# fp32 products on four column quarters, in a new order of operations: attention with memory, then a soft mixture of experts, on one core

## The chip, the core and the metric

The kernel runs on one core of a Trainium2 chip. The metric is the device time of one execution in microseconds. Before the change three runs gave 528.36, 534.36 and 540.67 us; the median is 534.36 us. One further execution was taken by the profiler and is the source of every row shown here.

## The reference

Everything is fp32. There are 8 batches, 8 heads, 576 positions and 64 features per head; then 8 experts of 4 slots each with a hidden width of 1024.

```python
scores = q @ k.T / 8, causal mask, softmax  -> a           # per (batch, head)
local  = a @ v
q_p    = where(q > 0, q, exp(q) - 1) + 1
mem    = (q_p @ M_prev) / (q_p @ z_prev + 1e-6)
attn   = sigmoid(beta) * mem + (1 - sigmoid(beta)) * local
x      = attn as (4608, 512)                               # heads side by side
logits = x @ phi                                           # 32 slots
d      = softmax of logits over the 4608 rows              # dispatch
slot_input = d.T @ x
slot_out[e] = relu(slot_input[e] @ w1[e]) @ w2[e]
out    = softmax of logits over the 32 slots @ slot_out    # combine
```

## The kernel before

**Attention.** Each of 32 iterations `n` handles one batch and a pair of heads, the two heads on the two halves of the 128 partitions. `loadq`, `loadk`, `loadv` and `loadm` fetch its inputs. `qhi`/`qlo` and `kn`/`kl` split q and k into a rounded part and a rest, from which `s.q1`, `s.q2` and `s.q3` make scores in three single-pass products (line 433, contraction over 64 partitions for each head). The blocks at the ends of the sequence, `s.a`, `s.b`, `s.z` and `s.zb`, are true fp32 products (line 427) with a stationary operand of 128 x 128. `max.*` (DVE, line 462) masks, scales and moves scores out of PSUM and finds the row minimum, `exp.*` (ACT) does the exponential with its sum, `t.*` transposes the result on the tensor engine (line 560), `te.*` moves the transposes out of PSUM into the tile `at`, and `av.*`/`memb` multiply by v (line 598), the two heads as two products with 64 columns each, side by side on the array.

**Memory part.** `qmin`, `qexp`, `qphi` make q_p. `norm` (line 518) makes its product with z, in four column quarters already. `neps`, `nmk`, `nred` work out the reciprocal in a form of 128 rows; `nrw` writes it to DRAM (line 540) and `nrr` reads it back, broadcast over rows, into the tile `rb` (line 546); `qn` (DVE, line 550) multiplies. `mema` multiplies by M (lines 592 and 593). In the same manner `rec`, `rt`, `rte` make the softmax reciprocal, `rrw` writes it to DRAM (lines 491 to 493), `rrr` reads it back as `rr`, a part of the tile `rm` (line 497), and `mo` (line 626) and `xe.*` (lines 633 to 637) combine everything into `xt`.

**Mixture.** For each block of 512 rows the operations `x1` to `x5` make logits, running maximum, dispatch sums and combine weights; `y*` is the last block and the hand-over. Then come the expert products `f1` and `f2` (lines 932 and 949, stationary operands of 32 columns, four experts side by side) and `comb` (line 1006), which also stores the output.

**What sets the order.** One string, `SEQ`, lists 2546 operations in program order, with the PSUM bank of each product after a colon (`t.1@5:0` is transposition 1 of iteration 5 into bank 0 of `psT`; there are three `psT` banks and two wider `psS` buffers). Every engine, and the SP queue, which issues nearly all transfers, takes its instructions in that order; `pin()` fixes it. `EV` says, for each movement out of PSUM and some elementwise steps, whether ACT, DVE or POOL (`a`, `v`, `p`) does it. `w@0` to `w@43` load 512 KB each of the expert weights during attention and just after; `WORD` says whether they go into memory of their own (-1) or into a tile that attention has given free. The tiles `rb`, `rr`, `rts`, `rn` and `at` exist once; q, k and scores exist twice, by the parity of n.

Of the kernel before, what the change touches and what calls it, by code (L numbers as in the profile page):

```python
# [51 lines left out]
neps@1 te.1@0 exp.b@1 nmk@1 rt@0:0 t.4@0:2 rte@0 qhi@2 max.q3h1@1 t.3@0:1 rrw@0 te.4@0 t.5@0:0 max.q3h0@1 exp.q2h1@1
s.z@1 te.3@0 exp.a@1 te.5@0 qn@0 s.a@2:1 s.zb@2 exp.q3h1@1 av.0@0 nred@1 rrr@0 max.z@1 av.2@0 kn@2 exp.z@1 loadk@3
av.1@0 loadq@3 max.a@2 kl@2 exp.q2h0@1 av.6@0 nrw@1 av.3@0 max.q1h0@1 exp.q3h0@1 memb@0:2 max.q1h1@1 s.b@2 loadv@1
mema@0:1 exp.q1h0@1 t.2@1:0 mo@0 qmin@2 loadm@2 s.z@2:0 nrr@1 te.2@1 xe.1@0 exp.q1h1@1 t.5@1:0 xe.0@0 qlo@2 t.1@1:1
rec@1 te.5@1 t.0@1:2 max.zb@2 max.b@2 qexp@2 rt@1:0 s.q2@2 rte@1 exp.a@2 qphi@2 rrw@1 te.1@1 s.q1@2 max.q2h1@2 te.0@1
t.4@1:0 max.q2h0@2 t.3@1:1 te.4@1 norm@2:2 te.3@1 neps@2 s.q3@2:1 rrr@1 exp.q2h0@2 nmk@2 max.q1h1@2 qhi@3 memb@1:0
kn@3 av.0@1 max.q1h0@2 loadq@4 qlo@3 exp.b@2 qn@1 exp.q1h0@2 av.3@1 max.z@2 av.6@1 exp.q2h1@2 kl@3 av.1@1 max.q3h0@2
exp.q1h1@2 av.2@1 nred@2 exp.q3h0@2 x3.0@0:1 nrw@2 exp.z@2 mema@1:2 mo@1 loadv@2 max.q3h1@2 loadk@4 s.q2@3:0 xe.1@1
nrr@2 exp.q3h1@2 s.q3@3:1 xe.0@1 x3e.0@0 rec@2 qmin@3 loadm@3 s.b@3 max.q3h1@3 t.4@2:2 qexp@3 max.q3h0@3 t.5@2:0  # L60
rt@2:1 s.zb@3 max.q2h1@3 te.5@2 s.q1@3:1 max.b@3 max.q2h0@3 exp.b@3 s.a@3 kn@4 rte@2 te.4@2 t.1@2:0 max.zb@3 rrw@2
qphi@3 t.0@2:1 kl@4 te.1@2 t.2@2:2 max.a@3 te.0@2 s.z@3 te.2@2 qn@2 exp.a@3 t.3@2:0 exp.q3h0@3 max.q1h0@3 mema@2:21
te.3@2 rrr@2 exp.q1h0@3 qhi@4 max.z@3 norm@3:0 qmin@4 loadm@4 av.0@2 neps@3 w@0 exp.q2h0@3 nmk@3 max.q1h1@3 av.3@2
nred@3 qlo@4 qexp@4 av.6@2 av.2@2 nrw@3 exp.q3h1@3 qphi@4 memb@2 av.1@2 loadk@5 exp.z@3 xe.0@2 s.q3@4:0 mo@2 nrr@3
exp.q1h1@3 exp.q2h1@3 s.q2@4:1 xe.1@2 rec@3 norm@4:0 loadv@3 max.q3h1@4 s.zb@4 neps@4 t.5@3:1 w@1 max.q3h0@4 t.3@3:2
te.5@3 loadq@5 s.b@4 te.3@3 rt@3:0 s.q1@4:0 rte@3 max.q2h1@4 rrw@3 x3.1@0:1 t.4@3:2 x3e.1@0 s.a@4 te.4@3 t.0@3:0 qn@3
t.1@3:1 te.0@3 max.q1h1@4 qhi@5 t.2@3:2 te.1@3 max.q2h0@4 s.z@4 qlo@5 rrr@3 exp.q2h1@4 nmk@4 max.q1h0@4 exp.q3h1@4
mema@3:10 nred@4 loadk@6 exp.q2h0@4 max.a@4 max.zb@4 kn@5 av.0@3 loadm@5 qmin@5 max.z@4 nrw@4 qexp@5 av.1@3 kl@5
te.2@3 max.b@4 av.3@3 qphi@5 exp.b@4 av.2@3 exp.z@4 memb@3 av.6@3 exp.q1h1@4 s.q2@5:0 loadv@4 mo@3 exp.q3h0@4 s.q3@5:1
xe.0@3 nrr@4 xe.1@3 exp.a@4 s.zb@5 max.q3h1@5 t.5@4:2 loadq@6 max.q3h0@5 x1.0@0:0 te.5@4 exp.q1h0@4 norm@5:1 x1.1@0  # L70
neps@5 rec@4 s.q1@5:1 x1l@0 nmk@5 rt@4:2 t.4@4:1 rte@4 max.zb@5 t.2@4:0 rrw@4 max.q2h1@5 te.4@4 t.3@4:2 qn@4 qhi@6
te.2@4 t.1@4:1 kn@6 exp.q3h1@5 x1m@0 s.a@5 t.0@4:0 te.3@4 te.1@4 s.z@5 te.0@4 max.q1h0@5 rrr@4 nred@5 x1e@0 s.b@5
mema@4:21 max.q2h0@5 exp.q2h1@5 qlo@6 exp.q3h0@5 x2@0:0 max.q1h1@5 loadm@6 qmin@6 memb@4 x2a@0 av.0@4 exp.q2h0@5
loadq@7 max.z@5 max.b@5 av.3@4 exp.z@5 kl@6 av.1@4 max.a@5 exp.a@5 av.6@4 xe.0@4 av.2@4 exp.q1h1@5 x2m@0 exp.b@5
s.q3@6:1 loadv@5 mo@4 exp.q1h0@5 qexp@6 s.q2@6:0 rec@5 loadk@7 xe.1@4 nrw@5 t.0@5:1 w@2 qphi@6 s.a@6 te.0@5 s.zb@6
rt@5:0 t.5@5:2 max.q3h0@6 rte@5 nrr@5 t.3@5:1 te.5@5 max.q3h1@6 s.b@6 t.1@5:0 x2e@0 te.3@5 te.1@5 s.q1@6:1 x2s@0
x4.0@0:2 qhi@7 norm@6:1 max.zb@6 x4a.0@0 x3.2@0:0 neps@6 max.a@6 max.q2h0@6 exp.q3h1@6 t.2@5:2 nmk@6 max.q1h0@6 x5@0:1
kn@7 s.z@6 x5e@0 max.b@6 te.2@5 max.q2h1@6 kl@7 x3e.2@0 qn@5 t.4@5:1 loadq@8 x3.3@0:2 te.4@5 rrw@5 nred@6 x3.0@1:0
exp.q3h0@6 max.q1h1@6 av.0@5 max.z@6 exp.b@6 exp.q2h1@6 x3e.3@0 nrw@6 memb@5:1 av.2@5 exp.z@6 qlo@7 av.6@5 rrr@5
av.1@5 exp.a@6 exp.q1h0@6 av.3@5 w@3 exp.q2h0@6 x4.1@0:2 nrr@6 exp.q1h1@6 x4a.1@0 s.q3@7:0 x3e.0@1 rec@6 s.q2@7:1  # L80
max.q3h0@7 loadk@8 max.q3h1@7 mema@5:2 mo@5 t.4@6:0 qmin@7 loadm@7 xe.1@5 s.a@7 loadv@6 te.4@6 s.zb@7 xe.0@5 s.q1@7:0
exp.q3h0@7 w@4 max.zb@7 max.q2h0@7 t.5@6:2 qhi@8 max.a@7 s.b@7 max.q2h1@7 te.5@6 rt@6:0 t.0@6:1 max.q1h1@7 kn@8 s.z@7
max.q1h0@7 rte@6 max.b@7 kl@8 qexp@7 te.0@6 rrw@6 t.1@6:2 qn@6 s.zb@8:1 te.1@6 t.3@6:0 qlo@8 max.z@7 t.2@6:1 x3.1@1:2
te.2@6 qphi@7 s.q3@8:0 exp.b@7 rrr@6 te.3@6 exp.q1h0@7 exp.q2h0@7 norm@7:1 max.q3h0@8 av.0@6 w@5 exp.q1h1@7 neps@7
nmk@7 loadq@9 exp.z@7 nred@7 av.3@6 w@6 av.1@6 max.q3h1@8 exp.a@7 nrw@7 exp.q2h1@7 loadk@9 x3e.1@1 av.6@6 av.2@6
exp.q3h1@7 memb@6:0 mema@6:1 loadv@7 mo@6 rec@7 s.b@8 xe.1@6 qmin@8 loadm@8 s.a@8 t.2@7:2 nrr@7 exp.q3h1@8 s.q1@8:0
te.2@7 s.q2@8 max.q1h0@8 xe.0@6 rt@7:1 kn@9 t.5@7:2 max.q2h1@8 rte@7 rrw@7 t.0@7:0 max.zb@8 kl@9 te.5@7 max.b@8
max.q1h1@8 s.z@8 exp.b@8 max.q2h0@8 te.0@7 max.a@8 t.1@7:1 qhi@9 max.z@8 qexp@8 t.3@7:2 qlo@9 exp.q1h1@8 s.b@9:1
qphi@8 t.4@7:0 rrr@7 te.3@7 qn@7 s.q3@9:0 te.4@7 te.1@7 w@7 norm@8:2 exp.q1h0@8 loadq@10 neps@8 av.0@7 exp.a@8
max.q3h0@9 loadk@10 nmk@8 exp.q3h0@8 max.q3h1@9 memb@7:0 av.1@7 exp.z@8 av.2@7 exp.q2h1@8 av.3@7 av.6@7 t.3@8:1 mo@7  # L90
mema@7:2 xe.1@7 s.q1@9:0 qmin@9 s.q2@9 te.3@8 xe.0@7 nred@8 exp.q2h0@8 x1.0@1:2 kn@10 max.q2h1@9 qexp@9 nrw@8 qhi@10
x1.1@1 max.q1h0@9 loadv@8 s.a@9 x1l@1 qlo@10 t.5@8:0 x1m@1 t.4@8:1 loadm@9 te.5@8 max.q2h0@9 kl@10 s.zb@9 w@8 t.2@8:2
x1e@1 te.4@8 nrr@8 t.1@8:0 exp.q1h0@9 rec@8 s.z@9 te.2@8 qphi@9 te.1@8 x2@1:1 max.a@9 max.zb@9 t.0@8:2 max.b@9 x2a@1
rt@8:0 te.0@8 s.q3@10:1 rte@8 exp.q3h1@9 rrw@8 max.z@9 exp.q2h1@9 x4.0@1:0 max.q1h1@9 norm@9:2 exp.b@9 neps@9 av.0@8
exp.q1h1@9 loadq@11 qn@8 nmk@9 loadk@11 exp.q2h0@9 av.3@8 x4a.0@1 rrr@8 exp.q3h0@9 memb@8:2 x2m@1 av.6@8 av.1@8
max.q3h0@10 exp.z@9 av.2@8 max.q3h1@10 exp.a@9 nred@9 s.q1@10:0 s.q2@10:1 rec@9 max.q1h1@10 x3.3@1:0 qhi@11 s.b@10
kn@11 x3e.3@1 mema@8:1 mo@8 exp.q3h0@10 kl@11 s.zb@10 loadm@10 max.q2h0@10 rt@9:0 s.z@10 rte@9 loadv@9 xe.0@8
exp.q1h1@10 qlo@11 xe.1@8 qmin@10 t.3@9:0 nrw@9 t.4@9:2 max.q1h0@10 rrw@9 te.3@9 s.a@10 te.4@9 qexp@10 t.1@9:1 t.0@9:0
te.1@9 max.a@10 max.zb@10 t.5@9:2 qphi@10 te.0@9 nrr@9 t.2@9:1 te.5@9 x1d@0 x3.2@1:0 max.b@10 max.q2h1@10 te.2@9
norm@10:2 rrr@9 max.z@10 av.0@9 neps@10 exp.q2h1@10 loadk@12 memb@9:1 exp.q1h0@10 av.3@9 loadq@12 av.2@9 x2e@1 x3e.2@1  # L100
av.1@9 qn@9 exp.q2h0@10 exp.a@10 x1d@1 av.6@9 nmk@10 exp.b@10 mema@9:2 nred@10 exp.q3h1@10 mo@9 nrw@10 t.3@10:0
# [1010 lines left out]
```

## Time and profile before

| | |
|---|---|
| median of three runs | 534.36 us |
| the profiled execution | 531.61 us, span 529.8 us |
| granted clock of the tensor engine in it | 0.963 |
| busy: PE, DVE, ACT, POOL | 462.5, 384.3, 342.4, 126.0 us |
| moved by DMA | 101.78 MB |

PE is the tensor engine's products, PEld its weight loads, DVE the vector engine, ACT the scalar engine, POOL GpSimd, and SPq the queue that issues transfers. In a row of a group, the numbers behind the bar are the busy time, the mean duration of one instruction in nanoseconds, and the idle time of the engine just before these instructions with what ended it. In a row of waits they are the total, the number of waits and the longest one. A true fp32 product makes two records on PE, one for each of two passes, and so does each quarter of one.

### The profile page before, as it was taken

How to read it: one execution, taken by the hardware profiler on the slowest of the kernel's cores; microseconds unless marked ns; L12 is line 12 of the kernel's file. 1: busy time of each engine (PE TensorE's matmuls, PEld its weight loads, DVE VectorE, ACT ScalarE, POOL GpSimd, SP SyncE). 2: the span in 40 equal slices, each digit the busy share in tenths (PEclk: the TensorE clock that was granted, in tenths of full speed). 3: DMA queues.
4: the chain of work that ended last, by engine and by line, in shares of the span. 5: the costliest groups of instructions: out<-in, count | busy, mean ns of one | idle time of the engine just before them, and what ended most of it. 6: DMA issues, size and time to landing. Idle time of an engine off the chain costs nothing.

```text
span 529.8 us, 11904 instructions
## 1 busy us (share of the span) xinstructions
PE 462.5 (87%) x3970; PEld 312.9 (59%) x3970; DVE 384.3 (73%) x1324; ACT 342.4 (65%) x985; POOL 126.0 (24%) x138
## 2 busy tenths in 40 slices
...
GB/s 198 178 143 132 191 158 150 209 191 188 142 200 146 137 136 171 143 147 128 188 123 171 185 182 162 83 233 117 158 203 125 218 196 168 379 415 408 222 337 323
DMA packets 66285, 101.78 MB, mean 192 GB/s; under 512 B 11248, under 2 KB 41520, under 8 KB 66224
## 3 DMA queue, kind: packets, MB, share of 16 engines
...
q14 instruction: 29, 0.24, 0.2%
...
HBM read 91.25 MB, written 9.73 MB: 191 GB/s over the span
## 4 chain that ended last, share of the span: by engine, by line
PE 36%; DMA 25%; DVE 21%; SPq 6%; ACT 5%; issue 4%; POOL 1%; DVEq 0%; POOLq 0%; ACTq 0%
PE oa L598 6%; PE psT L560 6%; DMA rb<-rd 5%; PE psS L433 5%; DVE q L462 4%; PE psS L427 4%; DMA rm<-rs 4%; DMA k<-in_k_dram 4%; DMA rd<-rq 3%; DVE zq L462 3%; PE pf L932 3%; DVE qp L550 3%; PE pc L1006 3%; PE psT L592 3%; DMA q<-in_M_dram 2%
## 5 line engine op out<-in xcount | busy, mean ns | idle before, releaser
L355 ACT COPY at<-psT 128x256 f32<-128x256 f32 (+1 forms) x202 | 86.5, 479 | 52.3 <-PE psT L560 49.1
L470 ACT ACTIVATE q<-q,nm 128x512 f32<-128x512 f32 (+2 forms) x160 | 97.6, 612 | 15.3 <-DVE nm L462 15.2
L598 PE MATMUL oa<-at,mv 128*64 128x320 f32 (+4 forms) x640 | 93.1, 427 | 3.0 <-DMA mv<-in_v_dram 1.3
L427 PE MATMUL psS<-k,qq 128*128 128x256 f32 (+2 forms) x320 | 69.2, 330 | 16.5 <-DVE nm L462 12.0
L462 DVE CUSTOM_DVE_ANT_0 q<-psS,mv 128x512 f32<-128x512 f32 (+1 forms) x128 | 76.1, 611 | 6.6 <-PE psS L433 3.9
L560 PE MATMUL psT<-cs,q 128*128 128x128 f32 x480 | 75.6, 282 | 2.8 <-DVE xt L633 1.1
L433 PE MATMUL psS<-K,X 64*128 64x512 f32 (+2 forms) x576 | 70.5, 365 | 8.5 <-DVE nm L462 6.1
L470 ACT ACTIVATE zq<-zq,nm 128x256 f32<-128x256 f32 (+2 forms) x128 | 67.7, 531 | 7.2 <-DVE nm L462 6.6
L427 PEld LDWEIGHTS psS<-k,qq 128*128 128x128 f32 x320 | 51.9, 199 | 28.3 <-DVE nm L462 17.6
L560 PEld LDWEIGHTS psT<-cs,q 128*128 128x128 f32 x480 | 58.0, 148 | 9.0 <-issue 2.3
L433 PEld LDWEIGHTS psS<-K,X 64*128 64x128 f32 x576 | 46.1, 188 | 26.9 <-issue 9.8
L598 PEld LDWEIGHTS oa<-at,mv 128*64 128x64 f32 x640 | 38.1, 137 | 38.0 <-issue 27.0
L560 PE MATMUL psT<-cs,zq 128*128 128x128 f32 x288 | 48.5, 283 | 2.3 <-DVE xt L633 0.9
L505 POOL TENSOR_SCALAR qp<-qq 128x576 f32<-128x576 f32 x19 | 31.8, 1676 | 74.0 <-PE psT L593 60.2
L550 DVE TENSOR_TENSOR qp<-qp,rb 128x576 f32<-128x576 f32 x32 | 27.0, 843 | 21.2 <-DMA rb<-rd 21.2
L626 DVE TENSOR_TENSOR xt<-oa,rm 128x448 f32<-128x448 f32 (+7 forms) x60 | 23.8, 435 | 24.2 <-DMA rm<-rs 18.1
L411 POOL TENSOR_TENSOR K<-k,K 128x512 fp32r<-128x512 f32 x25 | 32.8, 1314 | 31.3 <-ACT K L355 18.9
L358 DVE COPY at<-psT 128x512 f32<-128x512 f32 (+1 forms) x59 | 32.4, 570 | 10.1 <-PE psT L560 8.6
L592 PE MATMUL psT<-qp,q 128*128 128x512 f32 x64 | 35.1, 629 | 4.4 <-DVE qp L550 3.1
L560 PEld LDWEIGHTS psT<-cs,zq 128*128 128x128 f32 x288 | 34.8, 147 | 6.1 <-ACT at L355 1.1
L530 POOL TENSOR_TENSOR rn<-rn,rm 128x144 f32<-128x144 f32 x22 | 10.5, 477 | 91.3 <-ACT rn L523 57.9
L470 ACT ACTIVATION_READ_ACCUMULATOR q<-q,nm 128x1 f32 x160 | 31.0, 193 | 0.0
...
## 6 DMA issues: line engine op xcount, KB each, us to landing
...
```

The lines of the kernel that those rows point to most:

```text
L355: nc.scalar.copy(o, i)
L358: nc.vector.tensor_copy(out=o, in_=i)
L411: ALU_ENG[ev("kl", n)].tensor_tensor(out=K2[:, 1, :], in0=st[n]["k"][:, 0:512], in1=K2[:, 0, :].bitcast(F32), op=ALU.subtract)
L427: nc.tensor.matmul(ps[:, c + x0 - k0:c + x1 - k0], s["qd"][:, i], s["k"][:, x0:x1], start=True, stop=True)
L433: nc.tensor.matmul(ps[:, c0:c0 + N], X[ROW[h], x, 128 * i - 128:128 * i], K2[ROW[h], y, 0:N], start=(x, y) == (0, 0), stop=(x, y) == (0, 1))
L462: nc.vector.tensor_tensor_reduce(out=sm, in0=src, in1=msk, op0=ALU.add, op1=ALU.min, scale=-0.125, scalar=m0, accum_out=acc_o)
L470: nc.scalar.activation(sm, sm, AF.Exp, scale=-1.0, bias=s["nm"][:, J:J + 1], accum_out=s["sum"][:, J:J + 1])
L505: ALU_ENG[ev("qmin", n)].tensor_scalar(out=st[n]["qp"], in0=st[n]["q"], scalar1=0.0, scalar2=None, op0=ALU.min)
L550: ALU_ENG[ev("qn", n)].tensor_tensor(out=s["qp"], in0=s["qp"], in1=s["rb"], op=ALU.mult)
L560: nc.tensor.transpose(out=ps[:, 128 * x:128 * x + 128], in_=src[:, k0:k0 + 128], identity=ident)
L592: nc.tensor.matmul(om, s["m"][:, 0:128], s["qp"][:, 64:576], start=True, stop=True)
L598: nc.tensor.matmul(o[ROW[h], col:col + nx], vt[:, c, ROW[h]], at[:, a0 + hs * h:a0 + hs * h + nx], start=start, stop=stop)
```

## The change

A helper `quads` makes one product as four, each with 32 columns of the stationary operand, 32 rows of the output and the whole moving operand. It is used for `s.a`, `s.b`, `s.z`, `s.zb` and `mema`, which were one product with 128 columns, and for `av.*` and `memb`, which were two with 64 columns. Transpositions and the single-pass score products stay as they are. That is 33 more product instructions in each iteration.

`SEQ` holds the same 2546 operations in another order and with other PSUM banks. `EV` gives 29 movements and elementwise steps fewer to DVE (106 instead of 135), 23 more to ACT and 6 more to POOL. `WORD` and the places of `w@...` change too; `w@0` is now the fourth operation. The table shows how far apart in `SEQ` some steps of one iteration stand, in operations (smallest and median over the 32 iterations):

| from, to | before | after |
|---|---|---|
| `nrw` (write), `nrr` (read back) | 4, 10.5 | 18, 27 |
| `nrr`, `qn` | 20, 37.5 | 28, 46 |
| `rrw` (write), `rrr` (read back) | 13, 18 | 24, 36 |
| `rrr`, `mo` | 19, 29 | 26, 43 |
| `loadk`, `kn` | 16, 46 | 31, 52 |
| `loadm`, `norm` | 16, 34.5 | 22, 41.5 |
| `mema`, `xe.1` (a `psT` bank is held) | 1, 10.5 | 5, 25.5 |

On the tensor engine, going through `SEQ`, the shape of the array (whole, column halves, column quarters, row halves) changes 208 times before and 270 times after. Over all products, a `psT` bank is held for 3539 operations in sum before and 4154 after.

```diff
 SEQ = """
-gate@0 loadq@1 loadm@0 loadk@1 loadm@1 loadv@0 qhi@0 qmin@0 kn@0 s.zb@0:0 qlo@0 qexp@0 s.b@0 s.a@0 kl@0 qmin@1 qphi@0
-s.q3@0:1 max.b@0 max.a@0 exp.b@0 norm@0:0 max.q3h1@0 s.q2@0 neps@0 max.q3h0@0 exp.q3h1@0 nmk@0 max.q2h1@0 s.q1@0:1
...
+gate@0 loadm@0 loadq@1 w@0 loadm@1 loadv@0 loadk@1 qmin@0 qhi@0 qlo@0 qexp@0 kn@0 s.b@0:0 s.a@0 s.zb@0 kl@0 qphi@0
+qmin@1 s.q3@0:1 max.b@0 qexp@1 max.a@0 max.zb@0 norm@0:0 max.q3h0@0 neps@0 s.q2@0 max.q3h1@0 exp.b@0 nmk@0 exp.q3h0@0
...
 WORD = [-1, -1, -1, -1, -1, -1, -1, -1, -1, -1, -1, -1, -1, -1, -1, -1, -1, -1, -1, -1, -1, -1, -1, -1, -1, -1,
-        1, -1, 3, 5, 0, -1, 2, -1, 7, 11, 8, 14, 6, 4, 10, 9, 12, 13]
+        -1, -1, -1, 0, 2, 1, 3, 4, 6, 5, 7, 8, 11, 13, 14, 9, 10, 12]
...
+    def quads(o, w, x, start=True, stop=True):
+        for g in range(4):
+            nc.tensor.matmul(o[32 * g:32 * g + 32], w[:, 32 * g:32 * g + 32], x(g), start=start, stop=stop)
...
             for x0, x1 in zip(cuts, cuts[1:]):
-                nc.tensor.matmul(ps[:, c + x0 - k0:c + x1 - k0], s["qd"][:, i], s["k"][:, x0:x1], start=True, stop=True)
+                quads(ps[:, c + x0 - k0:c + x1 - k0], s["qd"][:, i], lambda g: s["k"][:, x0:x1])
...
         om = s["om"] = bank()
-        nc.tensor.matmul(om, s["m"][:, 0:128], s["qp"][:, 64:576], start=True, stop=True)
-        nc.tensor.matmul(ob(n)[:, 64:128], s["m"][:, 0:128], s["qp"][:, 0:64], start=True, stop=True)
+        quads(om, s["m"], lambda g: s["qp"][:, 64:576])
+        quads(ob(n)[:, 64:128], s["m"], lambda g: s["qp"][:, 0:64])
...
     def av_part(n, o, c, a0, nx, col, hs=512, start=False, stop=False):
-        for h in range(2):
-            nc.tensor.matmul(o[ROW[h], col:col + nx], vt[:, c, ROW[h]],
-                             at[:, a0 + hs * h:a0 + hs * h + nx], start=start, stop=stop)
+        quads(o[:, col:col + nx], vt[:, c], lambda g: at[:, a0 + g // 2 * hs:a0 + g // 2 * hs + nx], start=start, stop=stop)
```

More of the change, by code (lines that the diff above doesn't have):

```diff
@@ L52 @@
[L52 to L101, printed above, removed]
@@ new lines @@
+exp.a@3 t.5@2:1 loadk@5 qhi@4 nred@3 t.1@2:2 te.5@2 qlo@4 kl@4 t.4@2:0 nrw@3 te.1@2 loadq@5 t.2@2:1 max.z@3 te.4@2
+t.0@3:2 qn@2 te.2@2 s.a@4:1 s.b@4 exp.q1h0@3 s.zb@4 max.q1h1@3 av.0@2 exp.q1h1@3 rrr@2 mema@2:10 exp.z@3 te.0@3
+exp.b@3 max.zb@4 x3.1@0:2 loadm@4 rec@3 nrr@3 x3e.1@0 s.q2@4 qmin@4 max.q2h0@4 rt@3:2 av.6@2 rte@3 av.3@2 max.a@4
+qexp@4 rrw@3 max.q2h1@4 memb@2 av.1@2 exp.a@4 max.b@4 qphi@4 exp.b@4 av.2@2 t.5@3:2 loadv@3 te.5@3 s.q1@4:0 w@6
+s.q3@4:1 xe.0@2 mo@2 s.z@4 kn@5 xe.1@2 norm@4:2 loadq@6 t.3@3:0 max.q1h0@4 neps@4 t.2@3:1 nmk@4 rrr@3 te.3@3 t.4@3:2
@@ new lines @@
+t.0@6:1 loadq@9 te.4@6 qhi@8 max.q1h1@7 t.2@6:0 loadk@9 max.q2h1@7 te.0@6 kl@8 t.1@6:2 max.q2h0@7 te.2@6 x3.0@1:1
+max.q1h0@7 exp.q2h0@7 te.1@6 norm@7:0 qlo@8 av.0@6 max.a@7 max.z@7 exp.a@7 av.6@6 exp.q2h1@7 av.1@6 neps@7 x2s@0
+exp.q1h1@7 nmk@7 rrr@6 s.zb@8:1 av.3@6 exp.z@7 s.a@8 nred@7 s.q3@8:0 exp.q1h0@7 qn@6 nrw@7 x3e.0@1 t.1@7:2 w@8
+max.q3h1@8 x5@0:0 te.1@7 memb@6:1 av.2@6 max.q3h0@8 exp.b@7 mema@6:2 x5e@0 loadv@7 exp.q3h0@8 rec@7 rt@7:0 qmin@8
+loadm@8 rte@7 s.q1@8:0 max.zb@8 rrw@7 s.q2@8 max.q1h0@8 max.a@8 t.2@7:0 max.q2h0@8 kn@9 qexp@8 s.z@8 mo@6 nrr@7 qhi@9
```

373 lines of the change are left out of this document (207 added, 166 removed).

## The prediction

> **What bounds the kernel now.** I read the page first, then stretches, then waits, then the chain. The page says which engine is near its limit.
>
> ```profile
> span 529.8 us, 11904 instructions
> PE 462.5 (87%) x3970; PEld 312.9 (59%) x3970; DVE 384.3 (73%) x1324; ACT 342.4 (65%) x985; POOL 126.0 (24%) x138
> PE 36%; DMA 25%; DVE 21%; SPq 6%; ACT 5%; issue 4%; POOL 1%; DVEq 0%; POOLq 0%; ACTq 0%
> ```
>
> No engine is full, and a quarter of the chain that ended last lies in transfers. The stretches (columns: PE, PEld, DVE, ACT, POOL busy, then granted clock, DMA share and GB/s) separate attention from what follows.
>
> ```profile
> 20.00:440.00 420.00, 375.74 (x3148) 259.44 (x3149) 330.71 (x1182) 295.82 (x881) 116.61 (x122) 0.98 0.57 164
> 440.00:465.00 25.00, 21.08 (x244) 14.26 (x244) 13.16 (x41) 8.82 (x26) 1.06 (x1) 1.00 0.78 286
> 465.00:530.00 65.00, 49.36 (x480) 28.03 (x472) 25.47 (x46) 25.04 (x44) 0.00 (x0) 0.82 0.91 339
> ```
>
> In 420 us of attention PE has 375.7 us of records, so it stands still for 44.3 us, and DVE for 89.3 us. DMA is busy only 57% there: bandwidth isn't short, latency is. The expert part after 465 us is not touched by the change except through the weight loads. The waits say for which transfers (total, times, longest):
>
> ```profile
> DVE qp L550 <- DMA rb<-rd: 21.2, 15, 2.7
> DVE xt L626 <- DMA rm<-rs: 18.1, 10, 4.3
> PE psT L518 <- DMA q<-in_M_dram: 7.3, 4, 2.6
> PE psS L427 <- DMA k<-in_k_dram: 2.7, 1, 2.7
> SPq L546 <- DMA rd<-rq: 54.7, 27, 4.3
> SPq L497 <- DMA rs<-rts: 30.9, 29, 2.9
> ```
>
> DVE loses 21.2 + 18.1 = 39.3 us to the two read-backs from DRAM, PE 7.3 + 2.7 = 10.0 us to inputs. Two more rows explain why inputs are late at all: the SP queue itself stands for 54.7 + 30.9 = 85.6 us, because a read-back at its head waits for the write before it to land, and every load behind it stands too. In the chain the longest pieces of attention (start, length, what) are such transfers:
>
> ```profile
> 311.83 5.58 DMA rm<-rs
> 422.07 5.85 DMA q<-in_M_dram
> 436.30 5.00 DMA rb<-rd
> ```
>
> **The quarters.** How long products take is read from starts, since PE's ends are modelled. One stretch of the order of time on PE without idle time, and two pieces of the chain with products that are in quarters already:
>
> ```profile
> 202.54 0.29 PE L598 MATMUL psT<-at,mv 128*64 128x64 f32 x4
> 202.75 0.97 PE L433 MATMUL psS<-K,X 64*128 64x512 f32 x6
> 203.65 1.13 PE L592 MATMUL psT<-qp,q 128*128 128x512 f32 x2
> 204.61 0.33 PE L593 MATMUL psT<-qp,q 128*128 128x64 f32 x2
> 204.78 0.61 PE L560 MATMUL psT<-cs,q 128*128 128x128 f32 x4
> 205.22 0.56 PE L427 MATMUL psS<-k,qq 128*128 128x128 f32 x4
> ...
> 464.64 7.07 PE pf L932 x64
> ...
> 289.95 1.01 PE psT L646 x32
> ```
>
> A whole product of 512 columns takes 204.61 - 203.65 = 0.96 us just after a change of shape. In quarters, 64 records are 8 such products in 7.07 us, 0.88 us each. So for wide operands quarters stream at about the same pace, and a product gains at most 0.08 us. A whole product of 64 columns takes 204.78 - 204.61 = 0.17 us; the two halves of 64 columns take 202.75 - 202.54 = 0.21 us for both passes and a change of shape. Four transpositions take 205.22 - 204.78 = 0.44 us, 0.11 each, so a weight load of 128 columns sets a floor of 0.11 us for a pass. Without that floor, two passes over 64 columns at the pace of the 512 (0.88 / 8) take 0.11 us; 0.21 - 0.11 leaves 0.10 us for a change of shape, my estimate.
>
> `s.a`, `s.zb` and the small product of `mema` are 64 columns wide and whole: they save 0.17 - 0.11 = 0.06 us each, 3 x 32 x 0.06 = 5.8 us. Against that stand 62 more changes of shape, 62 x 0.10 = 6.2 us. PE is on the path for much of the time, so I take both in full: **+0.4 us**. Quarters as narrow as 64 columns are not in this trace. Their price lies between the pace above and that of the 128-column quarters at line 646, 1.01 us / 32 = 32 ns a record, hence 4 x 32 x 2 = 0.25 us for a product; the difference of 0.14 us falls on five products of an iteration (`s.a`, `s.zb`, `mema`, `av.6`, `memb`), at most 5 x 32 x 0.14 = 22.4 us. I take the lower end, since the halves of 64 columns are the nearest row. If wide quarters gave their 0.08 us each time, `s.z` and `mema` would give at most 3 x 32 x 0.08 = 7.7 us; I take none, as the 0.08 follows a change of shape, which stays.
>
> **The movements.** DVE gives up work. Durations by shape:
>
> ```profile
> L358 DVE COPY at<-psT 128x512 f32<-128x512 f32 x34 | 23.2, 681 | 7.5 <-PE psT L560 6.3 <-PE oa L598 1.1
> L358 DVE COPY at<-psT 128x256 f32<-128x256 f32 x25 | 9.4, 418 | 2.6 <-PE psT L560 2.3 <-ACT at L355 0.2
> L358 DVE COPY xk<-psT 128x512 f32<-128x512 f32 x12 | 8.1, 676 | 0.0
> L358 DVE COPY rts<-psT 9x128 f32<-9x128 f32 x14 | 3.9, 276 | 2.8 <-PE psT L481 2.5 <-DMA rd<-rq 0.2
> L525 DVE TENSOR_SCALAR rn<-psT,rm 128x144 f32<-128x144 f32 x12 | 4.4, 364 | 2.0 <-PE psT L518 1.9
> L358 DVE CAST X<-qq 128x384 fp32r<-128x384 f32 x9 | 5.6, 624 | 3.9 <-issue 1.8 <-DMA qq<-in_q_dram 1.4 <-PE psS L433 0.7
> L358 DVE CAST K<-k 128x512 fp32r<-128x512 f32 x6 | 2.5, 420 | 0.0
> L355 ACT COPY at<-psT 128x512 f32<-128x512 f32 x97 | 55.1, 588 | 31.2 <-PE psT L560 28.6 <-PE oa L598 1.4 <-DVE xt L633 0.9
> ```
>
> By the two lists, DVE loses 13 transposition copies of 512 (8.9 us), 4 of `te.4` as two copies of 256 (3.3), 6 `x3e` (4.1), 8 `rte` (2.2), 3 `qhi` (1.9) and 3 `kn` (1.3), and gets 9 `neps` (3.3): 18.4 us less. The chain has 21% in DVE, so I count 0.21 x 18.4 = **-3.9 us**; the ends are 0 and 18.4. ACT gets 23 more, at most 23 x 0.588 = 13.5 us; with 5% of the chain that is **+0.7 us**, and up to 13.5 us if ACT becomes the engine that PE's banks wait for (it idles 31.2 us before these very copies, for PE, which is its cover).
>
> **The order.** The 2546 operations end at about 465 us, 0.183 us each. Between `nrw` and `nrr` lie 10.5 operations (1.9 us) before and 27 (4.9 us) after; the queue waited 27 times for 54.7 / 27 = 2.0 us beyond the 1.9, so the write lands after some 3.9 us and the read-back now finds it done. Likewise `rrw` to `rrr`: 18 operations (3.3 us) and 30.9 / 29 = 1.1 us of wait make 4.4 us, against 36 operations, 6.6 us. The queue's 85.6 us of standing should mostly go, and inputs start earlier. On the reading side, `nrr` to `qn` grows by 8.5 operations, 1.6 us, against a mean wait of 21.2 / 15 = 1.4; `rrr` to `mo` by 14, 2.6 us, against 18.1 / 10 = 1.8. So most of DVE's 39.3 us of transfer waits go. How much of that is time? Nothing, where PE would have been late anyway; all of it and PE's 10.0 us, where nothing else is late. I take half of DVE's 39.3, **-19.7 us**, and none of PE's: DVE stands for 89.3 us in attention, less than half of it for transfers, and the rest will still be found, for PE and for ACT. What is late next is the tensor engine with its banks. `w@0` near the front puts 512 KB ahead of `loadm@1`, `loadv@0` and `loadk@1`, some 1.5 us at the 339 GB/s of the last stretch; I count nothing, since the first `kn@1` stands 40 operations (7 us) behind, and 1.5 us if that cover fails. Instructions on the SP queue stay as many; only their places move.
>
> The sum, on the profiled execution's own 531.61 us: 531.6 + 0.4 - 3.9 + 0.7 - 19.7 = 509.1. That execution is 0.5% under the median of the three runs, whose spread is 2.3%, so I don't correct for it: **509 us**.
>
> **Rivals.** (a) All goes: neither DVE nor PE waits for transfers. Then PE's records are the floor, and at most the 44.3 us of its idle time can go: 531.6 - 44.3 = 487 us. For it speaks that PE's waits behind DVE's row minima are themselves partly waits handed on; against it, that a fixed order always leaves some idle time. Chance 0.12.
>
> (b) The distances buy nothing: the waits for DRAM go, but DVE and PE now stand at the same places for one another, and the change does not do what its order says. Time 531.6 + 0.4 - 3.9 + 0.7 = 529 us. For it: PE and DVE are already busy 89% and 79% of attention, and the chain's pieces are many and short, so other paths lie close below. Against: the six wait rows above are large and direct. Chance 0.24.
>
> (c) Banks: to cover late read-backs the new order holds `psT` banks for 4154 operations in sum instead of 3539; `mema`'s waits 25.5 operations for `xe.1` instead of 10.5. That is 615 x 0.183 = 113 us of bank time, over three banks 38 us by which transpositions at line 560 could be held up. This is **slower**: taken whole with (b), 529 + 38 = 567 us; at half, 548. It decides once PE's idle time before line 560 passes the 19.7 us that the order saves. Today that row has almost none, so banks are no limit now:
>
> ```profile
> L560 PE MATMUL psT<-cs,q 128*128 128x128 f32 x480 | 75.6, 282 | 2.8 <-DVE xt L633 1.1 <-DVE xt L634 0.9 <-DVE r L475 0.4
> ```
>
> Held shares rise only from about 46% to 55%. Chance 0.10.
>
> (d) Four narrow quarters cost their upper price: 509.1 + 22.4 = 531.5 us. For it: no such row exists here; against: 64-column halves at full pace. Chance 0.06. The Trainium skill ("TensorE: Matmul & The Clock Gate", Part 3, the cost of a per-tile semaphore tail) says that each tile adds about 4.7 ns and each of its semaphore increments 26.3 ns; estimated from that, 33 more products in 32 iterations, all signalling, would cost 33 x 32 x 31 ns = 33 us and the sum would be 542. No row here shows how many of the four signal.
>
> **Numbers.** The forecast case has 0.48, (a) 0.12, (b) 0.24, (c) 0.10, (d) 0.06. What a measurement of this kernel can tell from no change is about 2%, 10.7 us around 534.4: faster is below 523.7, slower above 545.1. Forecast and (a) are faster, 0.60; (b) and (d) are the same, 0.30; (c) is slower, 0.10. The forecast's own range, with DVE's 39.3 us counted at a quarter to four quarters and the share of 18.4 us at its ends, is 490 to 523. For 8 in 10 the range takes in (b) and (d) with the spread of single runs, and (a) in part: **486 to 541**.
>
> **What would show it.** Right: SP's wait for `rd` falls from 54.7 to under 15 us, DVE's for `rb` and `rm` from 39.3 to under 12, DMA's share of the chain from 25% to under 15%; DVE's busy time is near 366, ACT's near 355. PE has 3970 + 33 x 32 x 2 = 6082 records at unchanged pace: an `s.a` in quarters starts the next product about 0.11 us later, without a change of shape. Wrong: transfer waits gone and the span unchanged, for (b); idle time at line 560 of more than 15 us, for (c); 0.25 us for a 64-column quarter product, for (d); DMA waits as large as before would break the step on distances.

## The result and the profile after

The changed kernel takes 488.17 us (median of four runs, 485.89 to 488.63); beside it the kernel before took 536.82 us. The ratio is 0.918 (95% interval 0.908 to 0.928): 8.2% less time, where 509 us had been forecast and 486 to 541 given as the range. Ratios here leave the executions of a second, slower state out, so a ratio is not always the quotient of two medians. The profiled execution took 485.89 us; the rows of after are from it.

The page of after: span, busy time of each engine, and the shares of the chain that ended last.

```profile
span 484.1 us, 16100 instructions
PE 446.6 (92%) x6082; PEld 277.1 (57%) x6082; DVE 368.8 (76%) x1290; ACT 350.3 (72%) x1013; POOL 124.8 (26%) x144
PE 59%; DVE 19%; DMA 9%; ACT 6%; issue 3%; SPq 1%; POOL 0%; DVEq 0%; ACTq 0%; POOLq 0%
```

The chain had 25% in transfers and 6% in the SP queue's own waits; it now has 9% and 1%, and 59% in PE instead of 36%. The stretches (PE, PEld, DVE, ACT, POOL busy, granted clock, DMA share, GB/s) of after, attention first:

```profile
20.00:420.00 400.00, 384.65 (x5469) 243.98 (x5467) 330.93 (x1199) 313.12 (x938) 119.80 (x132) 1.00 0.68 193
420.00:484.00 64.00, 46.91 (x480) 24.77 (x480) 25.30 (x47) 25.02 (x44) 0.00 (x0) 0.92 0.85 312
```

The expert products `f1` start at 420.00 us instead of 464.64, so 44.6 of the 45.7 us won from the span lie ahead of them, and the rest of the kernel lasts 64.1 us against 65.2. From 20 us up to that point PE had 375.74 + 21.08 = 396.8 us of records in 445 us before, and has 384.7 in 400 us now. So the gain there has two parts: PE stands still for 15.4 us instead of 48.2, **32.8 us**, and its records take **12.2 us** less. The waits of after (total, number, longest), the SP queue's among them, and the group of DVE at line 637, whose second wait is the read-back `rm`:

```profile
DVE qp L556 <- DMA rb<-rd: 6.7, 5, 3.9
PE psS L417 <- DVE nm L468: 4.5, 9, 1.6
SPq L552 <- DMA rd<-rq: 3.5, 3, 2.2
SPq L546 <- DVE rq L541: 33.4, 18, 4.3
```

```profile
L637 DVE TENSOR_TENSOR xt<-psT,rm 128x64 f32<-128x64 f32 x32 | 7.0, 217 | 3.2 <-PE psT L417 1.6 <-DMA rm<-rs 1.5
```

The queue's wait for `rd` fell from 54.7 to 3.5 us and the one for `rs` (30.9 us) is gone from the list; the largest sum that is left is the 33.4 us for DVE's `nred`, ahead of the write, which were 26.5 before. All waits of the queue up to `f1` together fell from 211.4 to 163.5 us. DVE's waits for read-backs fell from 39.3 to 6.7 + 1.5 = 8.2 us (and 0.2 at line 630, `mo`). The quarters as groups (busy, mean ns, idle before) and in time (start, length):

```profile
L417 PE MATMUL psS<-k,qq 128*32 128x64 f32 x512 | 18.0, 223 | 3.4 <-DVE nm L468 3.3
L566 PE MATMUL psT<-cs,q 128*128 128x128 f32 x480 | 72.6, 280 | 2.6 <-DVE xt L641 1.3 <-DVE rn L531 1.1
```

```profile
59.76 1.18 PE L417 MATMUL psT<-qp,q 128*32 128x512 f32 x16 [0.22 <-ACT at L356]
60.75 0.51 PE L417 MATMUL psS<-k,qq 128*32 128x64 f32 x16
...
62.59 0.29 PE L417 MATMUL psT<-at,mv 128*32 128x64 f32 x8
62.70 1.26 PE L417 MATMUL oa<-at,mv 128*32 128x448 f32 x16
```

A 64-column product in quarters (8 records) makes way for the next one after 62.70 - 62.59 = 0.11 us, as forecast. `mema` (16 records, 512 and 64 columns) takes 60.75 - 59.76 = 0.99 us; before, as two whole products, it took 204.78 - 203.65 = 1.13.

### The profile page after: what moved, and what is told of

Its sections match the earlier page's. It is cut to its first block, busy times and chain, and to the rows that moved or that the text cites. A ratio compares the mean times of both kernels' runs of the same rounds, so it can differ in the third digit from the quotient of the medians.

```text
span 484.1 us, 16100 instructions
## 1 busy us (share of the span) xinstructions
PE 446.6 (92%) x6082; PEld 277.1 (57%) x6082; DVE 368.8 (76%) x1290; ACT 350.3 (72%) x1013; POOL 124.8 (26%) x144
## 4 chain that ended last, share of the span: by engine, by line
PE 59%; DVE 19%; DMA 9%; ACT 6%; issue 3%; SPq 1%; POOL 0%; DVEq 0%; ACTq 0%; POOLq 0%
PE oa L417 12%; PE psT L566 11%; PE psS L439 10%; PE psS L417 6%; PE psT L417 6%; DVE q L468 3%; PE pf L936 3%; DVE zq L468 3%; DMA rm<-rs 2%; DMA mv<-in_v_dram 2%; DMA rb<-rd 2%; PE psT L716 2%; ACT w L356 2%; PE pc L1010 2%; DVE qp L518 2%
## 5 line engine op out<-in xcount | busy, mean ns | idle before, releaser
L356 ACT COPY at<-psT 128x512 f32<-128x512 f32 (+1 forms) x223 | 95.0, 483 | 35.9 <-PE psT L566 27.9
L417 PE MATMUL oa<-at,mv 128*32 128x320 f32 (+4 forms) x1280 | 98.4, 423 | 1.3 <-DMA mv<-in_v_dram 1.3
L476 ACT ACTIVATE zq<-zq,nm 128x64 f32<-128x64 f32 (+2 forms) x128 | 68.2, 538 | 8.2 <-DVE nm L468 7.8
L417 PE MATMUL psS<-k,qq 128*32 128x256 f32 (+2 forms) x1280 | 59.2, 297 | 4.6 <-DVE nm L468 4.5
L417 PEld LDWEIGHTS oa<-at,mv 128*32 128x32 f32 x1280 | 34.6, 110 | 30.0 <-issue 22.0
L417 PEld LDWEIGHTS psS<-k,qq 128*32 128x32 f32 x1280 | 32.6, 109 | 29.5 <-issue 11.1
L417 PE MATMUL psT<-qp,q 128*32 128x64 f32 (+1 forms) x512 | 37.3, 408 | 2.7 <-DVE qp L556 2.0
L361 POOL TENSOR_SCALAR K<-k 128x512 fp32r<-128x512 f32 x25 | 16.8, 673 | 77.1 <-PE psS L439 61.7
L412 POOL TENSOR_TENSOR K<-k,K 128x512 fp32r<-128x512 f32 x25 | 34.5, 1381 | 1.4 <-DVE K L359 0.4
L417 PEld LDWEIGHTS psT<-qp,q 128*32 128x32 f32 x512 | 15.2, 109 | 27.7 <-issue 22.0
L518 DVE SCALAR_TENSOR_TENSOR qp<-qq,qp 128x576 f32<-128x576 f32 x32 | 28.3, 885 | 3.2 <-ACT qp L514 3.2
```

The costliest lines, as they stand in the source:

```text
L356: nc.scalar.copy(o, i)
L361: ENG = dict(a=act, v=dve, p=lambda o, i: nc.gpsimd.tensor_scalar(out=o, in0=i, scalar1=1.0, scalar2=1.0, op0=ALU.mult, op1=ALU.mult))
L412: ALU_ENG[ev("kl", n)].tensor_tensor(out=K2[:, 1, :], in0=st[n]["k"][:, 0:512], in1=K2[:, 0, :].bitcast(F32), op=ALU.subtract)
L417: nc.tensor.matmul(o[32 * g:32 * g + 32], w[:, 32 * g:32 * g + 32], x(g), start=start, stop=stop)
L476: nc.scalar.activation(sm, sm, AF.Exp, scale=-1.0, bias=s["nm"][:, J:J + 1], accum_out=s["sum"][:, J:J + 1])
L518: ALU_ENG[ev("qphi", n)].scalar_tensor_tensor(out=t, in0=st[n]["q"], scalar=0.0, in1=t, op0=ALU.max, op1=ALU.add)
```

## The experiments

The theory after the result: the distances from write to read-back to use are worth nearly all of it, through the SP queue and through DVE together; the quarters little, the movements little. The rival: the quarters (fewer changes of shape, no floor of a 128-column weight load) make PE's work shorter and that is the gain.

### The order alone: the changed kernel with whole products and halves

```diff
-                quads(ps[:, c + x0 - k0:c + x1 - k0], s["qd"][:, i], lambda g: s["k"][:, x0:x1])
+                nc.tensor.matmul(ps[:, c + x0 - k0:c + x1 - k0], s["qd"][:, i], s["k"][:, x0:x1], start=True, stop=True)
...
-        quads(om, s["m"], lambda g: s["qp"][:, 64:576])
-        quads(ob(n)[:, 64:128], s["m"], lambda g: s["qp"][:, 0:64])
+        nc.tensor.matmul(om, s["m"][:, 0:128], s["qp"][:, 64:576], start=True, stop=True)
+        nc.tensor.matmul(ob(n)[:, 64:128], s["m"][:, 0:128], s["qp"][:, 0:64], start=True, stop=True)
...
-        quads(o[:, col:col + nx], vt[:, c], lambda g: at[:, a0 + g // 2 * hs:a0 + g // 2 * hs + nx], start=start, stop=stop)
+        for h in range(2):
+            nc.tensor.matmul(o[ROW[h], col:col + nx], vt[:, c, ROW[h]],
+                             at[:, a0 + hs * h:a0 + hs * h + nx], start=start, stop=stop)
```

> The new order, movements and weight places, with all products whole again (the two heads' products with v as two halves). Theory A, the distances between transfers and their users carry the gain: the transfer waits stay small as in the changed kernel, and PE pays 354 changes of shape instead of 270 (84 x 0.10 = 8.4 us) and the 5.8 us of the 64-column products, so 488 + 14 = 502 us. Theory B, the quarters carry the gain: most of it is lost, 520 us or more.

505.73 us, ratio 0.944 (0.938 to 0.950). Its page:

```profile
span 504.4 us, 11873 instructions
PE 473.7 (94%) x3970; PEld 305.8 (61%) x3970; DVE 369.6 (73%) x1290; ACT 351.1 (70%) x1013; POOL 123.8 (25%) x144
PE 77%; DVE 9%; DMA 6%; ACT 4%; issue 2%; SPq 1%; POOL 0%; ACTq 0%; DVEq 0%; POOLq 0%
```

Up to `f1` (columns as above):

```profile
20.00:437.30 417.30, 406.44 (x3399) 266.88 (x3398) 330.72 (x1197) 313.38 (x936) 118.43 (x131) 1.00 0.63 184
```

The order alone gives 5.6%, though with whole products it changes the array's shape 354 times instead of 208 and PE's records grow from 396.8 to 406.4 us. PE's idle time fell from 48.2 to 417.3 - 406.4 = 10.9 us, that is by 37.3. The chain has only 6% in transfers; 77% of it is PE. In this order the quarters are worth the remaining 505.7 - 488.2 = 17.5 us. "Order" stands here for all that `SEQ`, `EV` and `WORD` hold: the movements have a run of their own below, the places of the weights, the loads and the PSUM banks have none.

### The quarters alone: the kernel before with `quads`

The edit is the one above the other way round, in the kernel before.

> The kernel before with nothing changed but the products, in quarters. Theory A: transfer waits as before, 354 changes of shape instead of 208 (+14.6 us of PE) less 5.8 us for the 64-column products; PE isn't the only limit there, so 0 to 9 us slower than before, 535 to 546 us. Theory B: 515 us or less.

548.71 us, ratio 1.020 (1.012 to 1.029): some 2% slower, 2.7 us past the end of the range that was expected. The chain, the queue's wait, and the stretch up to `f1`:

```profile
PE 32%; DMA 27%; DVE 22%; SPq 7%; ACT 5%; issue 4%; POOL 1%; DVEq 0%; ACTq 0%; POOLq 0%
```

```profile
SPq L550 <- DMA rd<-rq: 57.2, 29, 4.8
```

```profile
20.00:480.73 460.73, 407.09 (x5424) 248.90 (x5417) 341.48 (x1223) 304.58 (x905) 117.77 (x123) 0.97 0.57 166
```

The rival falls: quarters alone bring no time. Of the profiled execution's loss, 10.3 us are longer records of PE (407.1 against 396.8) and 5.4 us idle time (53.6 against 48.2); half clock, 27.3 us of it up to `f1` against 17.1, accounts for at most 5.1 of the 10.3. In the old order they make 354 changes of shape against 208. That they cost 2% there and are worth 17.5 us in the new order fits one count: each order was laid out with few changes for its own form of product (208 whole, 270 quarters) and has 354 with the other's.

### One kind of product as halves again

The changed kernel with `av.*` and `memb` alone in two halves, as in the last part of the first diff. Changes of shape: 386 against 270.

> The changed kernel with only the products with v (av and memb) as two halves again. No product gets shorter or longer in streaming, but the array changes shape 386 times instead of 270. At 0.10 us each and with PE at its limit 6 to 12 us are lost, 494 to 500 us. If the quarters help by something other than changes of shape, the loss is under 4 us.

497.53 us, ratio 0.938 (0.932 to 0.944), 9.4 us more than the changed kernel. Up to `f1`:

```profile
20.00:430.96 410.96, 398.57 (x4700) 244.69 (x4698) 331.43 (x1199) 313.47 (x938) 119.46 (x132) 1.00 0.65 188
```

PE's records take 398.6 - 384.7 = 13.9 us more for 116 more changes, 0.12 us each, of which 9.4 / 116 = 0.08 us each became time. Not all of it need be the changes: a product of 512 columns took 0.91 us in halves and 0.86 in quarters where the next one had the same shape. The price of a change itself stands in rows of the kernel before (start, length, what):

```profile
62.31 0.28 PE L598 MATMUL psT<-at,mv 128*64 128x64 f32 x4
62.43 0.29 PE L598 MATMUL oa<-at,mv 128*64 128x64 f32 x4
62.64 1.49 PE L433 MATMUL psS<-K,X 64*128 64x384 f32 x12
```

Two halves of 64 columns make way after 62.43 - 62.31 = 0.12 us for a product of the same shape, and after 62.64 - 62.43 = 0.21 for one of another. That is 0.09 to 0.10 us for the change, and it shows that halves of 64 columns cost no more than quarters (0.11). So of the 17.5 us, 9.4 come from `av.*` and `memb` and 8.2 from `s.*` and `mema`. For the latter there are 32 changes fewer when they are whole, so the quarters themselves win more than 8.2 us there.

### The movements alone

The list `EV` of the changed kernel in the kernel before.

```diff
-        qmin@0 neps@0 te.2@0 te.0@0 neps@1 te.4@0 te.5@0 te.2@1 te.5@1 te.1@1 te.0@1 te.4@1 neps@2 kn@3 x3e.0@0 qmin@3 te.5@2
...
+        qmin@0 qmin@1 neps@0 te.2@0 te.0@0 rte@0 neps@1 te.5@0 te.3@0 te.2@1 te.1@1 qmin@2 te.4@1 te.5@1 te.3@1 x3e.0@0 te.3@2
...
```

> The kernel before with only the list of who moves what taken from the changed kernel (18 us less on DVE, 13 us more on ACT). Theory A: 0 to 5 us faster, 530 to 537 us. Theory C, relief of DVE carries a good part of the gain: 520 us or less.

The ratio is 1.001 (0.996 to 1.006). DVE's busy time fell as it should, from 384.3 to 369.3 us, and the time did not follow. This holds for the old order; no run takes the movements out of the changed kernel.

### The read-backs early again, in the changed kernel

`nrr` stands 10 operations behind `nrw` and `rrr` 18 behind `rrw`, as in the kernel before; the users stay where they are, and so are farther from the read-back. Nothing else moves. For the first iteration's `nrr`:

```diff
-exp.q2h1@0 s.zb@1 kl@1 qlo@1 w@1 exp.a@0 max.z@0 t.1@0:1 loadk@2 exp.q1h0@0 t.2@0:2 max.q1h1@0 exp.z@0 te.1@0 t.0@0:0
-exp.q1h1@0 qphi@1 s.q3@1:1 te.2@0 rec@0 nrr@0 s.q2@1 te.0@0 max.q3h1@1 rt@0:1 t.4@0:2 rte@0 max.q2h1@1 exp.q3h1@1
+exp.q2h1@0 nrr@0 s.zb@1 kl@1 qlo@1 w@1 exp.a@0 max.z@0 t.1@0:1 loadk@2 exp.q1h0@0 t.2@0:2 max.q1h1@0 exp.z@0 te.1@0
+t.0@0:0 exp.q1h1@0 qphi@1 s.q3@1:1 te.2@0 rec@0 s.q2@1 te.0@0 max.q3h1@1 rt@0:1 t.4@0:2 rte@0 max.q2h1@1 exp.q3h1@1
...
```

> The changed kernel with only the read-backs moved up in the order: nrr 10 operations behind nrw (27 in the changed kernel), rrr 18 behind rrw (36), as near as in the kernel before; their users then stand further behind them, not nearer. Theory A in its form with the queue (a read-back at the head of the SP queue waits for the write and holds up the loads behind it): the queue stands over 50 us for the writes again and the time rises by 10 to 25 us, 498 to 513 us. Theory D, the rest of the order carries the gain and a standing queue is harmless when loads are early: 493 us or less, with the queue standing all the same.

503.91 us, ratio 0.942 (0.936 to 0.948): 15.7 us are lost. The queue's waits, PE's waits for loads behind it, and DVE's for `rb`:

```profile
SPq L551 <- DMA rd<-rq: 62.6, 27, 3.8
SPq L502 <- DMA rs<-rts: 22.4, 25, 2.3
```

```profile
PE oa L416 <- DMA mv<-in_v_dram: 7.1, 6, 2.6
PE psS L416 <- DMA k<-in_k_dram: 2.5, 1, 2.5
PE psT L523 <- DMA q<-in_M_dram: 2.4, 2, 1.8
DVE qp L555 <- DMA rb<-rd: 4.8, 2, 2.9
```

The queue stands for 62.6 + 22.4 = 85.0 us again, as before the change (85.6). DVE waits no more for read-backs than in the changed kernel (8.0 us against 8.4, all rows), but PE waits 7.1 us for v, which it did for 1.3 us there, and 4.9 for k and M, for which it did not wait. With one more row of 1.0 for v that is 11.7 us more, out of 434.19 - 420.00 = 14.2 us by which `f1` starts later. So a queue that stands costs time by way of the loads behind it.

### The queue freed, in the kernel before

Each iteration reads back what the iteration before it wrote. The head's reciprocals are then another's: this part of the computation is changed, and with it the wait for the write is gone.

```diff
-            nc.sync.dma_start(out=rr[ROW[h]], in_=st[n]["rs"][h].rearrange("(o x) -> o x", o=1).broadcast_to([64, S]))
+            nc.sync.dma_start(out=rr[ROW[h]], in_=st[max(n - 1, 0)]["rs"][h].rearrange("(o x) -> o x", o=1).broadcast_to([64, S]))
...
-            src = st[n]["rd"][:, h, :].rearrange("g (o x) -> o g x", o=1).broadcast_to([64, 4, 144])
+            src = st[max(n - 1, 0)]["rd"][:, h, :].rearrange("g (o x) -> o g x", o=1).broadcast_to([64, 4, 144])
```

> The kernel before, but nrr and rrr read back what the iteration before wrote, so the reciprocals are those of another head and the queue has no write of its own iteration to wait for; order, transfers and sizes stay. The 85.6 us of standing for writes go to near 0. Theory A: the queue is one half of the story; moving the read-backs up in the changed kernel cost 15.7 us, so here 12 to 22 us are won, 512 to 523 us, with DVE's waits for rb and rm falling too because the read-backs start about 1 to 2 us earlier. Theory D: under 6 us.

515.88 us, ratio 0.968 (0.962 to 0.974): 0.032 x 533.9 = 17 us, near the 15.7 that the run above lost from the other side. The queue's waits for the two writes, and DVE's own waits:

```profile
SPq L497 <- DMA rs<-rts: 1.0, 1, 1.0
SPq L546 <- DMA rd<-rq: 0.5, 1, 0.5
```

```profile
DVE xt L626 <- DMA rm<-rs: 20.1, 9, 6.2
DVE qp L550 <- DMA rb<-rd: 10.6, 9, 3.2
```

The 85.6 us fell to 1.5, yet all waits of the queue up to `f1` only from 211.4 to 196.1: among others it now stands longer for the engines that make what is to be written (73.1 us at lines 491 and 540, 43.6 before). PE's waits for inputs fell from 11.3 to 5.0 us, DVE's for the read-backs from 39.3 to 30.7. So the 17 us are not the loads' alone, and that they come near 15.7 is in part chance. The cleaner figure for the **queue is the 15.7 us** of the run above, where DVE's waits stayed.

### The users near again, in the changed kernel

The read-backs are moved towards their users, so that `qn` stands 30 operations behind `nrr`, and `mo` and `xe.0` 24 behind `rrr`. The way from write to use keeps its length, and the queue keeps clear of the write. (`mo` and `xe.0` both use what `rrr` fetches; 24 is the distance to the nearer one.)

```diff
-exp.q1h1@0 qphi@1 s.q3@1:1 te.2@0 rec@0 nrr@0 s.q2@1 te.0@0 max.q3h1@1 rt@0:1 t.4@0:2 rte@0 max.q2h1@1 exp.q3h1@1
-rrw@0 norm@1:0 max.zb@1 s.b@1 max.q2h0@1 neps@1 t.3@0:1 max.q3h0@1 exp.q2h1@1 nmk@1 t.5@0:0 nred@1 exp.q3h0@1 s.z@1:1
+exp.q1h1@0 qphi@1 s.q3@1:1 te.2@0 rec@0 s.q2@1 te.0@0 max.q3h1@1 rt@0:1 t.4@0:2 rte@0 max.q2h1@1 exp.q3h1@1 rrw@0
+norm@1:0 max.zb@1 s.b@1 max.q2h0@1 neps@1 t.3@0:1 max.q3h0@1 exp.q2h1@1 nmk@1 nrr@0 t.5@0:0 nred@1 exp.q3h0@1 s.z@1:1
...
```

> The changed kernel with nrr and rrr moved down until qn stands 30 operations behind nrr (46 in the changed kernel) and mo or xe.0 24 behind rrr (43): the queue never waits for a write, but the users stand near. Theory A: DVE's waits for rb and rm rise from 8 to 20 us or more and the time by 6 to 20 us, 494 to 508 us. Theory D (what is won lies in the order of computing): 491 us or less.

521.5 us, ratio 0.970 (0.962 to 0.978). Against 0.918 that is 0.052 x 533.9 = 28 us lost, more than was expected. The chain and the waits, from an execution of 522.89 us:

```profile
PE 40%; DMA 24%; DVE 18%; SPq 6%; ACT 4%; issue 3%; POOL 1%; DVEq 0%; ACTq 0%; POOLq 0%
```

```profile
DVE xt L629 <- DMA rm<-rs: 18.6, 9, 5.1
DVE xt L636 <- DMA rm<-rs: 13.2, 11, 4.1
DVE qp L555 <- DMA rb<-rd: 11.0, 8, 2.5
```

DVE waits 18.6 + 13.2 + 11.0 = 42.8 us for the read-backs, 34.4 more than the 8.4 of the changed kernel. No row shows PE's products waiting for an input or the queue for either write, so this run holds the reader's side alone, as the run with the early read-backs held the queue's. Most of the wait becomes time; that it does so because little slack is left elsewhere is argued, not shown. 30 and 24 are shorter than the kernel before had in the median (37.5 and 29), so I take this as a bound from above for that side's share.

### The read-backs late, in the kernel before

The opposite trade: the queue is spared by putting `nrr` and `rrr` down to 26 and 24 operations behind their writes, which leaves 23.5 and 21 to the users.

```diff
-s.zb@1 exp.a@0 loadq@2 t.1@0:1 max.a@1 qexp@1 max.zb@1 qlo@1 max.q1h1@0 t.2@0:2 max.z@0 exp.q1h0@0 nrr@0 t.0@0:0
-te.2@0 max.b@1 s.q2@1 qphi@1 exp.z@0 s.q3@1:1 loadk@2 max.q2h1@1 exp.q1h1@0 max.q2h0@1 te.0@0 norm@1:2 rec@0 s.q1@1:0
+s.zb@1 exp.a@0 loadq@2 t.1@0:1 max.a@1 qexp@1 max.zb@1 qlo@1 max.q1h1@0 t.2@0:2 max.z@0 exp.q1h0@0 t.0@0:0 te.2@0
+max.b@1 s.q2@1 qphi@1 exp.z@0 s.q3@1:1 loadk@2 max.q2h1@1 exp.q1h1@0 max.q2h0@1 nrr@0 te.0@0 norm@1:2 rec@0 s.q1@1:0
...
```

> The kernel before with nrr and rrr moved down, towards their users, to 26 and 24 operations behind the writes (10.5 and 18 before), which leaves 23.5 operations from nrr to qn (37.5) and 21 from rrr to mo (29). Theory A: what the queue wins the users lose, since the way from the write to the user is as short as before; the queue's standing falls below 40 us, DVE's waits for rb and rm rise above 50 us, and the time stays within 530 to 548 us. If the queue alone decided: 517 us or less.

530.58 us, ratio 1.000 (0.993 to 1.008).

```profile
SPq L546 <- DMA rd<-rq: 23.8, 15, 3.9
SPq L497 <- DMA rs<-rts: 18.1, 22, 2.1
```

```profile
DVE qp L550 <- DMA rb<-rd: 28.0, 18, 3.0
DVE xt L626 <- DMA rm<-rs: 23.7, 16, 5.0
```

The queue's 85.6 us fell to 41.9 (under 40 had been expected), DVE's 39.3 rose to 51.7, and the time stayed. A read-back moved by itself only trades one wait for the other; what the changed kernel has besides is the longer way from `nrw` to `qn` and from `rrw` to `mo` as a whole (74 and 79 operations in the median, 49.5 and 46 before), and that needed the computation reordered. No run shortens both distances at once in the new order.

### Less work for PE, in both kernels

The third of the three score products is left out, in both kernels alike, so that part of the scores is missing; it is some 17 to 20 us of PE work (192 records).

```diff
-            for x, y in ((0, 0), (1, 0), (0, 1)):
+            for x, y in ((0, 0), (1, 0)):
...
-                                     start=(x, y) == (0, 0), stop=(x, y) == (0, 1))
+                                     start=(x, y) == (0, 0), stop=(x, y) == (1, 0))
```

> The kernel before without the third pass of the split score products (the product with the rest of k is left out), 32 x 0.52 = 17 us of tensor engine work less, everything else as it was. Theory A: PE isn't what decides here, 3 to 9 us are won, 526 to 532 us. If PE decided in the kernel before too, 14 us or more are won, 521 us or less.

> The changed kernel without the same third pass, 17 us of tensor engine work less. Theory A: with the transfer waits gone PE is the limit, so 11 to 17 us are won, 471 to 477 us. If another engine is the limit, under 6 us, 482 us or more.

Before: 536.03 us, ratio 1.006 (1.002 to 1.010), no gain at all. After: 480.11 us, 8 us under the changed kernel. Attention of the kernel before with less work:

```profile
20.00:440.00 420.00, 364.87 (x2930) 248.00 (x2926) 327.28 (x1167) 290.85 (x867) 115.71 (x121) 0.95 0.57 162
```

Both miss the figures that PE alone, or not at all, would give. Before, nothing was won, but the edit did not free 17 us: the granted clock fell from 0.98 to 0.95 in the same stretch, and PE's records there are only 375.7 - 364.9 = 10.9 us shorter. Those became idle time. After, PE is the main limit but passes on under half of what it is spared; the chain of that run has 27% in DVE against 19%.

### What is left in the tail

Behind `f1`, ACT makes eight casts `w` in a row, and DVE's subtraction takes what they write. One of each pair goes to POOL, behind the other cast:

```diff
-        act(o[0:32], w)
         act(o[64:96], w)
+        ENG["p"](o[0:32], w)
```

> The changed kernel with one of the two ACT casts of each combine weight piece (four of 1.04 us and four short ones, on the chain after the experts) given to POOL, which is idle then. Not part of the dispute; a version that may beat both. If ACT's eight long casts hold up g2 as the chain says, its copy comes about 4 us earlier, PE's idle time there of 3.7 us goes, and 3 to 5 us are won, 483 to 485 us; if the stores of the output set the end, under 1 us.

482.51 us (median of six), ratio 0.909 (0.904 to 0.915). The interval overlaps that of the changed kernel's 0.918, so the 5.7 us between the medians are likely but not settled. From `f1` to the end 61.6 us pass instead of 64.1, and PE's wait of 3.67 us there is gone. So 2.5 us lie where the edit is; the rest of the 5.7 has no cause that the runs show.

## Why the prediction was right, and where it was off

**The direction and the mechanism** stand. The conditions it set came out: SP's wait for `rd` 3.5 us (under 15), DVE's read-back waits 8.4 (under 12), DMA's share of the chain 9% (under 15), DVE busy 368.8 (near 366), ACT 350.3 (near 355), 6082 records on PE, 0.11 us for a quartered product of 64 columns. **The size** was off, and that 488.17 lies inside 486 to 541 owes something to luck: it is 2 us above the lower end and below the forecast's own 490 to 523. That 490 left out one of its own ends: with 39.3 us in full and the 18.4 us in full the sum is 531.6 + 0.4 + 0.7 - 39.3 - 18.4 = 475.

**The order: the step that failed in size** is "half of DVE's 39.3 us, and none of PE's 10.0". It gave 19.7 us. With whole products the new order took 37.3 us of PE's idle time away and made the kernel 5.6%, some 30 us, faster, though PE's records were 9.6 us longer. The reason given for the half, that DVE stands still for other causes which "will still be found", took DVE's idle time for the measure. In the changed kernel the near-users run shows otherwise: 34.4 us more of DVE's read-back waits cost some 28 us, not half. And the queue's share came in separately, by PE's late loads: 15.7 us. The two sides, 16 and up to 28 us, can't be added, as the late-read-back run shows that they trade against each other. How the gain of the order splits between them, and what the moved loads, weights and banks add, stays open.

**Clock**, a term that the prediction did not have: five stretches of half clock in attention before, none after (below). Five times 3.4 us at half speed are at most 8.5 of the 12.2 us by which PE's records became shorter.

**The quarters: +0.4 us** was two terms, and the theory with which the runs began, that the quarters are worth little, was wrong for the new order. The price of a change of shape, 0.10 us by estimate, is what the rows show (0.09 to 0.10). The gain was too small. `mema` as a whole gained 1.13 - 0.99 = 0.14 us, so some of the 0.08 of a wide product, "I take none", is there; two products of 256 columns at line 427 gained none (0.87 us whole, 0.86 to 0.89 in quarters). The 64-column products of line 427 mostly took 0.17 to 0.27 us whole, in quarters 0.11 to 0.14, so 0.06 us each is the lower end. The reason given for that gain, "a floor of 0.11 us for a pass" by a weight load of 128 columns, is not shown: the whole 64-column product needed 0.17 us for two passes, less than two such floors, and 0.11 us is just what 128 columns take at the prediction's own pace of 0.88 / 8 for 64 columns in two passes. As a sum, in the new order quarters shorten PE's records by 406.4 - 384.7 = 21.7 us at full clock in both, of which 17.5 became time. The comparison with the old order's 208 changes was right for the change as made, but hid that the new order needs the quarters. In the old order the prediction's terms give 146 x 0.10 - 5.8 = 8.8 us of loss on PE, and its records became 10.3 us longer, some of it clock; so that loss is mostly the changes too.

**DVE's 18.4 us at 21%, -3.9 us,** was wrong: the busy time fell by 15 us in the run with the movements alone, and the time by nothing that its interval, 0.996 to 1.006, would show. So a share of the chain was no exchange rate for busy time here. That what was taken off stood beside waits is argued.

**The rivals.** (a), "all goes", said 487 us and is the closest; it had 0.12. It took the 44.3 us of PE's idle time as what can go at most, and the number is nearly right by luck: 15.4 us of idle time remain, and records 12.2 us shorter made up for most of them. (b) falls with the chain's 59% in PE and the time. (c), banks, falls: PE's idle time at the transpositions (line 566) is 2.6 us, though the banks are held longer. (d) falls by 0.11 us a product. The estimate from the Trainium skill ("TensorE: Matmul & The Clock Gate", Part 3) beside it, 33 us more for the tiles' semaphore tails and 542 us in sum, is not borne out: with 2112 more records the same order is 17.5 us faster than with whole products. The 33 us assumed that every product signals, which no row here shows.

**The chances.** 0.60 for faster was held down by (b) at 0.24. The page spoke against (b) more than that: transfers and the queue's waits held 25% and 6% of the chain itself, so they weren't idle time beside another limit.
